# Expert weights loaded as paced halves, and shifted value tiles built without moving partitions

## The chip, the core and the metric

The kernel runs on one core of a Trainium2 chip. The metric is the device time of one execution in microseconds (us). Besides the DMA queues the core has five engines that the text names: PE (TensorE, the matrix multiplier; PEld is its weight load), DVE (VectorE), ACT (ScalarE), POOL (GpSimd) and SP (SyncE, which here only issues DMAs).

## What is computed

Three layers in float32, one after the other. Sizes: 4 batches, 8 heads, 512 local and 32 global tokens of 64 dimensions; 8 experts with 4 slots each; a last layer of width 2048.

```python
# 1. attention: a local token sees the 32 global tokens and the local ones within 32 positions
mask = np.abs(pos[:, None] - pos[None, :]) <= 32
s_ll = np.where(mask, scale * q_l @ k_l.T, -1e9)
a_l = softmax(concat([scale * q_l @ k_g.T, s_ll]))
out_l = a_l @ concat([v_g, v_l])          # global tokens see everything: out_g
# 2. soft mixture of experts on x (2176 tokens of 512)
logits = x @ phi
slot_input = softmax(logits, axis=0).T @ x
slot_out[e] = relu(slot_input[e] @ w1[e]) @ w2[e]
x = softmax(logits, axis=1) @ slot_out
# 3. last layer
out = relu(x @ w_in) ** 2 @ w_out
```

w_in and w_out are float64 in memory and are taken apart on the chip.

## The kernel before

**Stages.** The attention takes the first 166 us, the experts' matmuls follow up to about 202, and from there to the end (434 us) the last layer runs. The change touches the attention stage only, and the loading of expert weights that runs under it.

**Attention.** The 32 pairs of batch and head fall into 8 groups g of four heads (NG = 8), and the 512 query rows of a group into 4 units uu of 128 rows. That gives 32 steps n = 4g + uu. A unit has 16 / 4 = 4 blocks i of 32 queries; block i looks at a window of three key blocks x0, x0+1, x0+2 with x0 = first_block(i), and at the 32 global keys, 128 score columns in all. `emit_S` (L358) makes the scores on PE (32 matmuls of 32 x 128 a step), adds the mask on DVE (L376) and exponentiates on ACT (L380). `emit_T` transposes the result on PE (L388) and copies it on ACT. `emit_PV` multiplies by the values (L400) and divides on DVE (L407 to L409). `glob_S`, `glob_T` and `glob_PV` do the global queries (L423 to L471).

**Keys and values.** Keys lie in `kT` as six frames f of 128 columns: 32 global keys, then 96 local ones (three blocks). A window that starts inside a frame runs on into the next frame, whose global columns then stand in its middle: a contiguous run of 128 columns from 32 * (4f + (0, 2, 3)[x % 3]) holds the window, with its blocks rotated, and the mask is rotated likewise in `constants` (L293). Values lie in `v_e` the same way, by partitions: frame f has the global values on partitions 0 to 31 and three local blocks on 32 to 127. For a window with x % 3 == 0 the frame itself serves. For the others a shifted copy is made whose rows are in the order of the score columns: `prep_win` (x % 3 == 1, POOL, L343 and L344, two copies of 64 partitions) and `prep_win2` (x % 3 == 2, two windows at once, DVE, L350 and L352, four copies of 32 partitions x 520 numbers, each to another 32 partitions than it reads). `prep_win2` runs twice a group, so 16 times and 64 copies in all.

**Order of work.** Each piece is entered with a number (`at(when, ...)`), and the sorted list is the program order of PE, ACT, DVE, POOL and SP alike; nothing is reordered later. The unit of `when` is a step. In a group, counted from 4g, the loads of queries and keys for heads to come stand at 0.455 (first pair of heads, `load0`) and at 2.906 (second pair, right after `sort0`, the DVE copy L242 that reads the first pair at 2.901); the load of values stands at 3.675 (SP for the global part, POOL for the local one). A load that waits on SP holds up every load behind it.

**Expert weights.** 32 tiles of 1 MB, listed in `specs` in the order in which the experts use them. The first 13 go to slots of a ring that are free from the start (`more_weights`, L153), at the steps of the table WAT plus 0.9: 2.9, 3.9, 5.9, 7.9, 9.9, 10.9, 13.9, 14.9, 15.9 (twice), 18.9, 19.9 (twice). The next ones take slots that the attention gives back (`release`: three at 25.85, and so on).

Of the kernel before, what the change touches and what calls it, by code (L numbers as in the profile page):

```python
# [9 lines left out]
F32 = mybir.dt.float32  # L10
# [48 lines left out]
EX = 'act'  # L59
EE = 'act'  # L60
EW = 'act'
WAT = [2, 3, 5, 7, 9, 10, 13, 14, 15, 15, 18, 19, 19]
RECTS = 'A0-1 B0-2 C0-4 A2-6 B3-8 C5-10 A7-12 B9-15 A13-15 C11-15'
RING = 13
MORE = 5
# [8 lines left out]
def kernel(  # L74
# [7 lines left out]
    nc = tc.nc  # L82
    const = ctx.enter_context(tc.tile_pool(name="const", bufs=1))
    ring = ctx.enter_context(tc.tile_pool(name="ring", bufs=RING, side="right"))
# [19 lines left out]
    specs = []  # L104
    for kind, q in UNITS:
        es = slice(2 * q, 2 * q + 2)
        for m in range(4):
            src = (
                w1[es, m * 128:(m + 1) * 128, :].rearrange("e p f -> p e f") if kind == "w1" else
                w2[es, m * 256:(m + 1) * 256, :].rearrange("e (p t) d -> p e (t d)", t=2)  # L110
            )
# [4 lines left out]
    wt, raw = {}, {}  # L116
    w_in32, w_out32 = w_in.bitcast(I32), w_out.bitcast(I32)
    st = {"next": 0, "limit": RING}

    def slot(tag, shape, dt, nm):  # L120
        return ring.tile(shape, dt, tag=tag, name=nm, bufs={"w": RING, "k": MORE, "m": LAST}[tag])

    def load_raw(f, tag="k", halves=(0, 1)):
        if 0 in halves:
            raw[f] = slot(tag, [128, 2048], I32, "raw")
            nc.sync.dma_start(
                out=raw[f][:, 0:1024].rearrange("p (k w) -> p k w", k=4),
                in_=w_in32[:, 256 * f:256 * f + 256].rearrange("(k p) w -> p k w", p=128),
            )
        if 1 in halves:  # L130
            nc.sync.dma_start(out=raw[f][:, 1024:2048], in_=w_out32[128 * f:128 * f + 128, :])

    def more_weights(n=1):
        for _ in range(n):
            i = st["next"]
            if i >= len(specs) or i >= st["limit"]:
                return
            key, src = specs[i]
            if i == ALL:

                wt[key] = bp.tile([128, NT * 128], F32, tag="cT", name="extra")[:, 0:2048].rearrange(
                    "p (e f) -> p e f", e=2
                )
                nc.sync.dma_start(out=wt[key], in_=src)
                st["next"] += 1
                continue
            j = (i - (i > ALL)) % ALL
            if key[0] == "raw":
                load_raw(0, "w", [key[1]])
                st["next"] += 1  # L150
                continue
            t = slot("w" if j < RING else "k" if j < RING + MORE else "m", list(src.shape), F32, f"ring{i}")
            nc.sync.dma_start(out=t, in_=src)  # L153
            wt[key] = t
            st["next"] += 1

    def release(n):
        st["limit"] += n
        more_weights(n)
# [27 lines left out]
    kT, qT, v_e, kgT, qgT = [[], []], [[], []], [None] * 2, {}, {}  # L187
# [26 lines left out]
    pt_buf, win = [None] * 2, {}  # L214
# [4 lines left out]
    win = {x: w.rearrange("p (h d) -> p h d", d=65) for x, w in win.items()}  # L219
# [62 lines left out]
    def first_block(i):  # L282

        return min(max(i - 1, 0), 13)

    def constants(uu):

        for s in range(4):
            i = 4 * uu + s
            x0 = first_block(i)  # L290
            rows = slice(32 * s, 32 * s + 32)
            for x in range(x0, x0 + 3):
                c = (1 + x % 3 - (0, 2, 3)[x0 % 3]) % 4  # L293
                t = mask[rows, uu, 32 * c:32 * c + 32]
                if abs(x - i) > 1:
                    nc.gpsimd.memset(t, BIG)
                elif x != i:
                    nc.gpsimd.affine_select(
                        out=t, in_=t, pattern=[[i - x, 32]], compare_op=ALU.is_ge, fill=BIG, base=0,
                        channel_multiplier=x - i,  # L300
                    )
# [38 lines left out]
    def prep_win(g, x):  # L340

        ve, f = v_e[g % 2], x // 3
        nc.gpsimd.tensor_copy(win[x][0:64], ve[64:128, f])  # L343
        nc.gpsimd.tensor_copy(win[x][64:128], ve[0:64, f + 1])  # L344

    def prep_win2(g, k):
        ve, f = v_e[g % 2], 2 * k
        t = win2[1 if g == NG - 1 else k]
        win.update({3 * f + 2: t[:, 0], 3 * f + 5: t[:, 1]})
        nc.vector.tensor_copy(t[0:32], ve[96:128, f:f + 2])  # L350
        for c in range(3):
            nc.vector.tensor_copy(t[32 * c + 32:32 * c + 64], ve[32 * c:32 * c + 32, f + 1:f + 3])  # L352

    xb = {}
    P_t, PT_t = {}, {}

    def emit_S(g, uu):
        n = 4 * g + uu  # L358
        pt = p_buf[n % 2].rearrange("p (h x) -> p h x", h=4)
        nm = ap2.tile([128, 4], F32, tag="nm", name="nm", bufs=3)  # L360
        ps = [ps_s.tile([128, 2, 128], F32, tag="S", name="s") for _ in range(2)]
        for p in range(2):
            for hx in range(2):
                rows = slice(64 * hx, 64 * hx + 64)
                for s in range(4):
                    i = 4 * uu + s
                    x = first_block(i)
                    k0 = 32 * (4 * (x // 3) + (0, 2, 3)[x % 3])
                    nc.tensor.matmul(  # L369
                        ps[hx][32 * s:32 * s + 32, p, :],  # L370
                        qT[g % 2][p][rows, 32 * i:32 * i + 32], kT[g % 2][p][rows, k0:k0 + 128],
                        start=True, stop=True,
                    )
        for h in range(4):
            dst = pt[:, h, :]
            nc.vector.tensor_tensor_reduce(  # L376
                out=dst, in0=ps[h % 2][:, h // 2, :], in1=mask[:, uu, :], scale=1.0, scalar=FAR,
                op0=ALU.add, op1=ALU.min, accum_out=nm[:, h:h + 1],
            )
            nc.scalar.activation(out=dst, in_=dst, func=AF.Exp, bias=nm[:, h:h + 1], scale=-1.0)  # L380
        P_t[n] = pt
# [258 lines left out]
    load_global(k_g, "kg_sb")  # L640
    nc.gpsimd.memset(mask, 0.0)
    constants(0)
    ones()
    for uu in range(1, 4):
        constants(uu)
# [32 lines left out]
    def at(when, fn, *args):  # L678
        order.append((when, len(order), fn, args))

    steps = 4 * NG
    for n in range(steps):
        g, uu = n // 4, n % 4
        at(n - 2 + 0.1, emit_S, g, uu)
        at(n - 1 + 0.2, emit_T, g, uu)
        at(n + 0.6, emit_PV, g, uu)
    for g in range(NG):
        b, gq = g // 2, g % 2
        a = lambda name: 4 * g + (LASTPOS.get((name, g)) or POS[name])
        for p in range(2):  # L690
            for i, name in enumerate("qk"):
                at(-3 + 0.2 * p + 0.1 * i if g == 0 else a(f"sort{p}"), sort_qk, g, p, i)
            if (g, p) == (0, 0):
                at(-2.5, prep_global, "kg_sb", kg2, 1.0)
            for i, fn in enumerate((prep_q, prep_k)):
                at(-3 + 0.2 * p + 0.1 * i + 0.05 if g == 0 else 4 * g - 4 + p + 0.3 + 0.1 * i, fn, g, p)
            if g:
                at(-2.75 if (g, p) == (1, 0) else a("load0") if p == 0 else a("sort0") + 0.005, load_qk, g, p)
        at(a("glob_S"), glob_S, g)
        at(a("glob_T"), glob_T, g)  # L700
        at(a("glob_PV"), glob_PV, g)
        if g + 2 < NG:
            at(a("glob_PV") + 0.02, load_v, g + 2)
        for x in (1, 4, 7, 10, 13):
            at(a(f"w{x}"), prep_win, g, x)
        for k in range(2):
            at(a(f"v{k}"), prep_win2, g, k)
        if gq == 0:
            continue
        for uu in range(4 if g < NG - 1 else 2):  # L710
            at(a(f"x{uu}"), lambda b=b, uu=uu: x_T(b, uu, xb[(b, uu)], uu in (0, 3)))
        if g < NG - 1:
            at(a("L"), logits, b, b == 0, [(lt_all[:, b, :], slice(0, 128))])
            at(a("E"), slot_E, b)
            at(a("sl"), lambda b=b: slots(b, [xb[(b, uu)] for uu in range(4)]))
# [5 lines left out]
    at(2.19, slot_sums)  # L721
    at(steps - 2 + 0.8, lambda: x_T(B - 1, "g", x_g))
    at(steps - 1 + 0.5, last_xT, B - 1)
    for when in WAT:
        at(when + 0.9, more_weights)
    for when, n in RELEASE:
        at(when, release, n)
    for when, n in BUSYS:
# [163 lines left out]
    t = slot("m", [128, 4, 512], I32, "sgvm")  # L892
# [127 lines left out]
    t = slot("m", [128, 4, 512], I32, "sgvm2")  # L1020
# [169 lines left out]
    for n in range(len(seq)):  # L1190
        credit = min(credit + RATE, 1.2)
        if pieces and n >= START and min(free) <= n:
            kind, f, a, fs = pieces[0]
            if n >= due[kind, f] or (credit >= 1 and not ntile[max(n - 1, -1)]):
                d = 2
# [4 lines left out]
                d = min(d, late)  # L1200
# [59 lines left out]
```

## Time and profile before

| | us |
|---|---|
| median of 3 runs | 432.5 (431.55 to 434.31) |
| the profiled execution, its own time | 436.24 |
| its span, first to last instruction | 434.3 |
| PE busy / DVE busy / ACT busy / POOL busy in the span | 397.0 / 306.9 / 291.7 / 69.2 |
| mean granted clock of PE | 0.981 |

Busy is time in which an engine works on something; a wait or an issue of a DMA is not counted. Matmuls are pipelined and their ends are modelled, so a busy PE need not be at its peak. [...] In the views a row names the line, the engine, the operation, and the tile that is written and those that are read (out<-in).

### The profile page before, as it was taken

To read this page: it belongs to the slowest core of one execution; us is meant where nothing else is said; L and a number is where in the kernel's file an instruction comes from. 1 tells how busy PE (TensorE), PEld (TensorE's weight loads), DVE (VectorE), ACT (ScalarE), POOL (GpSimd) and SP (SyncE) were. 2 spreads that over 40 slices of the span, in tenths; PEclk is the share of its full clock that TensorE was granted. 3 is DMA by queue.
4 is the path that set the end of the run, shared out by engine and by line. 5 is a ranking of instruction groups with operands and counts; after the bars stand their busy time and mean duration, and the time that the engine had idled before them with its cause. 6 is when DMAs were issued, how large, how long until landed. Compare 5 with 4: busy or idle time off the path is not lost.

```text
span 434.3 us, 11765 instructions
## 1 busy us (share of the span) xinstructions
PE 397.0 (91%) x4530; PEld 289.9 (67%) x4530; DVE 306.9 (71%) x928; ACT 291.7 (67%) x692; POOL 69.2 (16%) x169
## 2 busy tenths in 40 slices
PE   6968888887889889999889999999999999999995
PEld 5747565564566654335667777878788787888883
DVE  2878779775987852436989996897788686735523
ACT  3556777693778761114888898878689786866670
POOL 7326346261743201000000000000000000000000
PEclk9988999996999999999999999999999999999998
DMA  7667696786878698999622232314020000003303
GB/s 184 148 197 208 213 296 204 261 223 236 200 225 258 217 361 339 394 407 375 230 98 97 78 117 54 140 26 169 0 97 2 0 1 2 0 2 145 138 9 121
DMA packets 46247, 70.29 MB, mean 162 GB/s; under 512 B 16336, under 2 KB 32720, under 8 KB 46192
## 3 DMA queue, kind: packets, MB, share of 16 engines
q1 hardware_dynamic: 44560, 66.40, 45.2%
q0 software_dynamic: 1632, 3.15, 3.1%
q8 instruction: 36, 0.59, 0.5%
q14 instruction: 19, 0.16, 0.1%
HBM read 65.08 MB, written 4.46 MB: 160 GB/s over the span
## 4 chain that ended last, share of the span: by engine, by line
PE 69%; DVE 11%; ACT 8%; DMA 5%; issue 4%; SPq 1%; POOL 0%; DVEq 0%; ACTq 0%; POOLq 0%
PE ops L1063 14%; PE ops L1064 14%; PE ops L1065 14%; PE hps L1028 4%; DMA qk<-in_k_l_dram 4%; PE hp L841 3%; PE so L869 3%; PE X L400 2%; PE s L369 2%; DVE tbuf L352 2%; ACT pbuf L380 2%; PE pT L388 2%; DVE pbuf L376 2%; DVE qk L242 1%; DMA v<-in_v_g_dram 1%
## 5 line engine op out<-in xcount | busy, mean ns | idle before, releaser
L1063 PE MATMUL ops<-hl,gh 128*128 128x512 f32 x266 | 105.8, 398 | 0.1
L1064 PE MATMUL ops<-hl,gh 128*128 128x512 f32 x266 | 105.5, 397 | 0.0
L1065 PE MATMUL ops<-hl,gl 128*128 128x512 f32 x266 | 105.0, 395 | 0.4 <-DVE gl L1052 0.4
L1052 DVE TENSOR_TENSOR gl<-r,gh 128x384 fp32r<-128x384 f32 x96 | 50.0, 531 | 28.1 <-ACT r L1047 27.9
L380 ACT ACTIVATE pbuf<-pbuf,nm 128x128 f32<-128x128 f32 x128 | 40.9, 390 | 34.1 <-DVE nm L376 33.7
L1035 ACT ACTIVATE r<-hps 128x384 f32<-128x384 f32 x96 | 45.1, 470 | 24.6 <-PE hps L1028 23.2
L1065 PEld LDWEIGHTS ops<-hl,gl 128*128 128x128 f32 x266 | 50.1, 188 | 13.2 <-DVE gl L1052 0.9
L1063 PEld LDWEIGHTS ops<-hl,gh 128*128 128x128 f32 x266 | 49.9, 188 | 12.1 <-ACT oacc L1075 0.7
L1064 PEld LDWEIGHTS ops<-hl,gh 128*128 128x128 f32 x266 | 50.0, 188 | 8.0
L1047 ACT ACTIVATE r<-r 128x384 f32<-128x384 f32 x96 | 48.7, 507 | 3.0
L1043 ACT ACTIVATE gh<-r 128x384 fp32r<-128x384 f32 x96 | 48.6, 506 | 2.6
L1028 PE MATMUL hps<-cT,wst 128*128 128x384 f32 x96 | 33.6, 353 | 2.1 <-ACT r L1035 2.0
L376 DVE CUSTOM_DVE_ANT_0 pbuf<-s,tbuf 128x128 f32<-128x128 f32 x128 | 29.4, 286 | 8.3 <-PE s L369 7.1
L1079 DVE SCALAR_TENSOR_TENSOR oacc<-ops,oacc 128x512 f32<-128x512 f32 x38 | 24.7, 686 | 4.1 <-PE ops L1065 4.0
L921 DVE SCALAR_TENSOR_TENSOR sgvm<-raw,sgvm 128x512 int32<-128x512 int32 x32 | 22.0, 686 | 5.3 <-ACT sgvm L915 5.3
L388 PE MATMUL pT<-ident,pbuf 128*128 128x128 f32 x128 | 22.1, 298 | 2.9 <-ACT tbuf L163 2.9
L1028 PEld LDWEIGHTS hps<-cT,wst 128*128 128x128 f32 x96 | 17.9, 188 | 9.5 <-ACT r L1035 2.7
L257 POOL DMA_DIRECT2D v<-in_v_l_dram x36 | 23.7, 665 | 0.0
L915 ACT ACTIVATE sgvm<-sgvm,ebias 128x512 int32<-128x512 int32 x32 | 22.8, 712 | 0.5 <-DVE sgvm L909 0.3
L918 DVE SCALAR_TENSOR_TENSOR sgvm<-raw,sgvm 128x512 f32<-128x512 uint32 x32 | 22.0, 686 | 0.1
L388 PEld LDWEIGHTS pT<-ident,pbuf 128*128 128x128 f32 x128 | 14.5, 147 | 9.1 <-ACT tbuf L163 3.9
L976 DVE TENSOR_TENSOR wst<-wpr,misc 128x256 fp32r<-128x256 f32 (+1 forms) x10 | 3.7, 372 | 18.3 <-ACT misc L971 18.3
(201 smaller groups left out, 710.2 us busy)
## 6 DMA issues: line engine op xcount, KB each, us to landing
ring<-in_moe_w_dram SPq DMA_DIRECT2D x31, 1024.0 KB, 8.6
raw<-in_moe_w_in_dram SPq DMA_DIRECT2D x16, 512.0 KB, 4.2
raw<-in_moe_w_out_dram SPq DMA_DIRECT2D x16, 512.0 KB, 5.0
out_dram<-oacc SPq DMA_DIRECT2D x16, 256.0 KB, 2.1
qk<-in_q_l_dram SPq DMA_DIRECT2D x15, 256.0 KB, 3.5
qk<-in_k_l_dram SPq DMA_DIRECT2D x15, 256.0 KB, 4.4
v<-in_v_l_dram POOLq DMA_DIRECT2D x30, 96.0 KB, 4.7
v<-in_v_g_dram SPq DMA_DIRECT2D x48, 32.0 KB, 3.9
```

Of the source, the lines that this page charges most:

```text
L376: nc.vector.tensor_tensor_reduce(out=dst, in0=ps[h % 2][:, h // 2, :], in1=mask[:, uu, :], scale=1.0, scalar=FAR, op0=ALU.add, op1=ALU.min ...
L380: nc.scalar.activation(out=dst, in_=dst, func=AF.Exp, bias=nm[:, h:h + 1], scale=-1.0)
L388: nc.tensor.transpose(ps[:, 128 * h:128 * h + 128], pt[:, h, :], ident)
L1028: nc.tensor.matmul(ps, wst[:, f, :], cT[:, t0:t0 + n], start=True, stop=True)
L1035: nc.scalar.activation(out=r, in_=ps, func=AF.Relu)
L1043: nc.scalar.activation(out=gh, in_=r, func=AF.Square)
L1047: nc.scalar.activation(out=r, in_=r, func=AF.Square)
L1052: eng.tensor_tensor(out=gL, in0=sq, in1=gh.bitcast(F32), op=ALU.subtract)
L1063: nc.tensor.matmul(ob[tt], gh[:, s], hi, start=first, stop=False)
L1064: nc.tensor.matmul(ob[tt], gh[:, s], lo, start=False, stop=False)
L1065: nc.tensor.matmul(ob[tt], gL[:, s], hi, start=False, stop=last)
L1079: nc.vector.scalar_tensor_tensor(out=t, in0=ps, scalar=WS, in1=t, op0=ALU.mult, op1=ALU.add)
```

## The change

Four edits that hang together.

1. **Value tiles.** In `prep_win` and `prep_win2` a row of values stays on its partitions: the blocks that lie in the next frame are copied from there, the others from this frame. `prep_win2` needs two copies (96 and 32 partitions) in place of four, 32 in all in place of 64; `prep_win` still takes two.
2. **Score columns.** The rows of the value tiles now stand in the order global, block 0, 1, 2 of a frame, so the score columns must too. `window_keys` reads the keys for a window with x % 3 == 1 as two runs of 64 columns and for x % 3 == 2 as four runs of 32, the later address first (steps of -64 and -96). Of the 16 blocks of a group 6 have x % 3 == 0 and stay one run, 6 have two runs and 4 have four. The mask goes to the same columns in `constants`.
3. **Expert loads.** The 13 loads of the ring become 26 loads of half a tile (0.5 MB; `ring_halves`). The table PACE puts them later: from step 4.9 to 25.71 where WAT had 2.9 to 19.9. In each group k = 1 to 5 one half stands at 4k + 0.9, two at 4k + 1.71, and two (k = 1, 2) or one (k = 3 to 5) at 4k + 2.76; four more halves follow at 24.9 and 25.71.
4. **Pacing.** The halves at .71 and .76 wait for POOL: a memset of one number in the slot stands ahead of each in POOL's order, and SP's load waits for it.

```diff
--- before.py
+++ after.py
@@ -59,7 +59,8 @@
 EX = 'act'
 EE = 'act'
 EW = 'act'
-WAT = [2, 3, 5, 7, 9, 10, 13, 14, 15, 15, 18, 19, 19]
+PACE = [(4 * k + d, n, w) for k in range(1, 6) for d, n, w in ((0.9, 1, False), (1.71, 2, True), (2.76, 2 if k < 3 else 1, True))]
+PACE += [(24.9, 2, False), (25.71, 2, True)]
 RECTS = 'A0-1 B0-2 C0-4 A2-6 B3-8 C5-10 A7-12 B9-15 A13-15 C11-15'
 RING = 13
 MORE = 5
@@ -154,6 +155,24 @@
             wt[key] = t
             st["next"] += 1
 
+    part = {}
+
+    def ring_halves(n, paced):
+
+        for _ in range(n):
+            key, src = specs[st["next"]]
+            c = part.get("c", 0)
+            if c == 0:
+                part["t"] = slot("w", list(src.shape), F32, f"ring{st['next']}")
+            t = part["t"]
+            if paced:
+                nc.gpsimd.memset(t[0:1, c, 0:1], 0.0)
+            nc.sync.dma_start(out=t[:, c:c + 1], in_=src[:, c:c + 1])
+            part["c"] = 1 - c
+            if c:
+                wt[key] = t
+                st["next"] += 1
+
     def release(n):
         st["limit"] += n
         more_weights(n)
@@ -290,7 +309,7 @@
             x0 = first_block(i)
             rows = slice(32 * s, 32 * s + 32)
             for x in range(x0, x0 + 3):
-                c = (1 + x % 3 - (0, 2, 3)[x0 % 3]) % 4
+                c = 1 + x % 3
                 t = mask[rows, uu, 32 * c:32 * c + 32]
                 if abs(x - i) > 1:
                     nc.gpsimd.memset(t, BIG)
@@ -340,19 +359,26 @@
     def prep_win(g, x):
 
         ve, f = v_e[g % 2], x // 3
-        nc.gpsimd.tensor_copy(win[x][0:64], ve[64:128, f])
-        nc.gpsimd.tensor_copy(win[x][64:128], ve[0:64, f + 1])
+        nc.gpsimd.tensor_copy(win[x][0:64], ve[0:64, f + 1])
+        nc.gpsimd.tensor_copy(win[x][64:128], ve[64:128, f])
 
     def prep_win2(g, k):
         ve, f = v_e[g % 2], 2 * k
         t = win2[1 if g == NG - 1 else k]
         win.update({3 * f + 2: t[:, 0], 3 * f + 5: t[:, 1]})
-        nc.vector.tensor_copy(t[0:32], ve[96:128, f:f + 2])
-        for c in range(3):
-            nc.vector.tensor_copy(t[32 * c + 32:32 * c + 64], ve[32 * c:32 * c + 32, f + 1:f + 3])
+        nc.vector.tensor_copy(t[0:96], ve[0:96, f + 1:f + 3])
+        nc.vector.tensor_copy(t[96:128], ve[96:128, f:f + 2])
 
     xb = {}
     P_t, PT_t = {}, {}
+
+    def window_keys(kt, x):
+
+        f, r = x // 3, x % 3
+        if not r:
+            return kt[:, 128 * f:128 * f + 128]
+        dims = [[-64, 2], [1, 64]] if r == 1 else [[-64, 2], [-96, 2], [1, 32]]
+        return bass.AP(kt.tensor, kt.offset + 128 * (f + r), [list(kt.ap[0])] + dims)
 
     def emit_S(g, uu):
         n = 4 * g + uu
@@ -364,11 +390,9 @@
                 rows = slice(64 * hx, 64 * hx + 64)
                 for s in range(4):
                     i = 4 * uu + s
-                    x = first_block(i)
-                    k0 = 32 * (4 * (x // 3) + (0, 2, 3)[x % 3])
                     nc.tensor.matmul(
                         ps[hx][32 * s:32 * s + 32, p, :],
-                        qT[g % 2][p][rows, 32 * i:32 * i + 32], kT[g % 2][p][rows, k0:k0 + 128],
+                        qT[g % 2][p][rows, 32 * i:32 * i + 32], window_keys(kT[g % 2][p][rows], first_block(i)),
                         start=True, stop=True,
                     )
         for h in range(4):
@@ -721,8 +745,8 @@
     at(2.19, slot_sums)
     at(steps - 2 + 0.8, lambda: x_T(B - 1, "g", x_g))
     at(steps - 1 + 0.5, last_xT, B - 1)
-    for when in WAT:
-        at(when + 0.9, more_weights)
+    for when, n, paced in PACE:
+        at(when, ring_halves, n, paced)
     for when, n in RELEASE:
         at(when, release, n)
     for when, n in BUSYS:
```

Three places show how the instructions move.

DVE, in the steps of group 5 (heads 4 to 7 of batch 2). The line numbers of the changed file are 19 to 24 higher; q_99 is a slot that holds a shifted value tile (win2), v_104 a frame tile of values. Before:

```order
L376 ISA nm 128x1
L350 COPY q_99<-v_104 32x520
L352 COPY q_99<-v_104 32x520 x3
L407 TENSOR_SCALAR rc<-X 128x4
L408 RECIPROCAL rc<-rc 128x4
```

and after the change:

```order
L400 ISA nm 128x1
L369 COPY q_99<-v_104 96x520
L370 COPY q_99<-v_104 32x520
L431 TENSOR_SCALAR rc<-X 128x4
L432 RECIPROCAL rc<-rc 128x4
```

Four copies are two, one of them three times as tall; what stands ahead and behind is the same.

SP, from the load of global values for group 6 to the next load of values. qk is the one buffer for queries and keys as loaded, ring_N is a weight slot. Before:

```order
L254 DMA v_100<-in_v_g_dram 32x4x64 x6
L153 DMA ring_2271<-in_moe_w_dram 128x2x1024
L153 DMA ring_2273<-in_moe_w_dram 128x2x1024
L235 DMA qk<-in_q_l_dram 128x2x256
L235 DMA qk<-in_k_l_dram 128x2x256
```

(then the same two qk loads for the second pair of heads, and L254 again). After:

```order
L273 DMA v_100<-in_v_g_dram 32x4x64 x6
L254 DMA qk<-in_q_l_dram 128x2x256
L254 DMA qk<-in_k_l_dram 128x2x256
L170 DMA ring_2342<-in_moe_w_dram 128x1024 x2
L170 DMA ring_2418<-in_moe_w_dram 128x1024 x2
```

(then the second pair's qk loads and L273). Two weight tiles that stood ahead of the first pair's load now stand behind it, and ahead of the second pair's.

POOL, in the same group. The tiles named gbuf, tbuf and v_104 hold value windows made by prep_win. Before:

```order
L343 COPY v_104<-v_104 64x260
L344 COPY v_104<-v_104 64x260
L431 MEMSET gbuf 128x5x32
L343 COPY gbuf<-v_100 64x260
L344 COPY gbuf<-v_100 64x260
```

and after:

```order
L362 COPY v_104<-v_104 64x260
L363 COPY v_104<-v_104 64x260
L169 MEMSET ring_2342 1x1
L169 MEMSET ring_2418 1x1
L455 MEMSET gbuf 128x5x32
L362 COPY gbuf<-v_100 64x260
L363 COPY gbuf<-v_100 64x260
L169 MEMSET ring_2418 1x1
```

The three memsets are what three of the four halves of that group wait for, so these halves leave SP when POOL has come that far.

## Rows read from the trace of the kernel before

**Rows 1.** The page: the profiled span.

```profile
span 434.3 us, 11765 instructions
```

**Rows 2.** Busy time in three stretches; the last columns are clock, DMA share, GB/s.

```profile
10.00:165.90 155.90, 130.67 (x3146) 93.97 (x3145) 121.62 (x543) 105.27 (x313) 60.04 (x126) 0.96 0.74 235
165.90:202.00 36.10, 35.88 (x297) 12.41 (x297) 14.33 (x59) 7.30 (x12) 1.52 (x2) 1.00 0.98 376
210.00:434.30 224.30, 216.18 (x994) 171.04 (x986) 163.07 (x313) 170.48 (x352) 0.00 (x0) 0.99 0.20 68
```

**Rows 3.** Waits of PE from 10 to 166: us in total, times, longest.

```profile
PE X L400 <- DVE xb L409: 2.6, 3, 1.5
...
PE s L369 <- issue: 2.2, 1, 2.2
...
PE X L400 <- issue: 1.6, 2, 0.9
...
PE Xg L459 <- issue: 1.4, 1, 1.4
```

**Rows 4.** DVE's copies by form, 10 to 166: count | busy us, mean ns | idle before.

```profile
L352 DVE COPY tbuf<-v 32x520 f32<-32x520 f32 x27 | 14.6, 540 | 0.5
...
L242 DVE COPY qk<-qk 128x512 f32<-128x512 f32 x28 | 11.6, 453 | 0.3 <-DMA qk<-in_k_l_dram 0.3
...
L352 DVE COPY q<-v 32x520 f32<-32x520 f32 x21 | 10.4, 496 | 0.3
...
L350 DVE COPY tbuf<-v 32x520 f32<-32x520 f32 x9 | 4.6, 511 | 0.3
...
L350 DVE COPY q<-v 32x520 f32<-32x520 f32 x7 | 3.1, 444 | 0.2
```

**Rows 5.** Timeline of DVE, one call of prep_win2: start us, us.

```profile
29.24 0.57 DVE L350 COPY q<-v 32x520 f32<-32x520 f32 x1
29.82 1.63 DVE L352 COPY q<-v 32x520 f32<-32x520 f32 x3
```

**Rows 6.** Chain that ended last, 10 to 166, share of it by line.

```profile
by line: issue 10.5%; DMA qk<-in_k_l_dram 10.0%; PE X L400 6.4%; PE s L369 6.1%; DVE tbuf L352 5.8%; ACT pbuf L380 4.5%; PE pT L388 4.5%; DVE pbuf L376 4.5%; DVE qk L242 3.0%; DMA v<-in_v_g_dram 3.0%; PE sl L548 3.0%; PE sg L423 2.5%; PE Xg
```

**Rows 7.** SP's timeline, the chain and DVE's timeline around one load of keys.

```profile
113.50 1.12 SPq L153 DMA_DIRECT2D ring<-in_moe_w_dram  x2
...
116.23 9.91 DMA qk<-in_k_l_dram
...
126.17 0.59 DVE L242 COPY qk<-qk 128x512 f32<-128x512 f32 x1 [0.26 <-DMA qk<-in_k_l_dram]
```

**Rows 8.** A stop of PE: its timeline, busy time after it, DMA queues 96 to 101.

```profile
100.69 1.11 PE L369 MATMUL s<-keys,pbuf 64*32 64x128 f32 x32 [2.19 <-issue]
...
102.00:104.00 2.00, 2.00 (x37) 1.49 (x37) 1.94 (x11) 1.76 (x5) 0.03 (x1) 0.50 0.98 381
...
q8 instruction: 1, 0.02, 1.4%
```

**Rows 9.** Matmuls by form, 43.6 to 145.7, and 166 to 202 (L869).

```profile
L369 PE MATMUL s<-keys,q 64*32 64x128 f32 x384 | 9.7, 276 | 2.6 <-ACT xT L163 2.6
...
L423 PE MATMUL sg<-keys 64*32 64x480 f32 x56 | 7.1, 575 | 0.0
...
L869 PE MATMUL so<-ring,hTz 128*32 128x512 f32 x128 | 15.7, 598 | 0.0
```

**Rows 10.** Timelines of POOL, SP and DVE around one second-pair load.

```profile
49.36 0.40 POOL L344 COPY gbuf<-v 64x260 f32<-64x260 f32 x1
...
50.66 0.37 SPq L235 DMA_DIRECT2D qk<-in_q_l_dram  x1
...
57.69 0.96 DVE L242 COPY qk<-qk 128x512 f32<-128x512 f32 x2
```

**Rows 11.** The page: loads to landing; busy time 140 to 150.

```profile
qk<-in_k_l_dram SPq DMA_DIRECT2D x15, 256.0 KB, 4.4
...
140.00:150.00 10.00, 8.92 (x261) 5.49 (x250) 8.44 (x42) 7.19 (x21) 2.65 (x7) 1.00 0.66 254
```

## The prediction, made before the changed kernel was timed

> **What bounds the kernel now.** I read the span first [rows 1], then the busy time by stage [rows 2]. The reader is to see three stages with different limits. From 210 to the end PE is busy 216.2 of 224.3 us, with the DMA at 0.20: the last layer is PE's, and no instruction of it changes. From 166 to 202 PE is busy 35.9 of 36.1 us while the DMA works at 0.98: PE is fed just fast enough. So only the attention can give something: 155.9 us in which PE is busy 130.7 and DVE 121.6. Neither is full; they take turns being late, since every step passes from PE to DVE to ACT and back to PE. PE's idle time there is 155.9 - 130.7 = 25.2 us, and that is the most that the change can give as long as PE's own work stays as it is.
>
> PE's waits divide this [rows 3]. Three rows, 2.2 + 1.6 + 1.4 = 5.2 us, end in "issue": PE stood still though no semaphore held it. The other 20.0 us are mostly waits for DVE and ACT, such as 2.6 us for the division on DVE (L409). DVE's value copies stand ahead of it. They are 64 copies, 14.6 + 10.4 + 4.6 + 3.1 = 32.7 us, 0.51 us each [rows 4], and they come as a block of four, 29.24 to 31.45, in front of the division [rows 5]. The chain of work that ended last passes through the copies of one line into one tile for 5.8% of 156 us, 9.0 us of the 14.6 us that these copies are busy [rows 4, 6].
>
> **The change part by part.**
>
> Value copies. 32 copies go, 32 stay. The trace has no copy of 96 partitions; bounds for it are the shortest mean of the 32-partition copies, 0.444 us, and the longest, 0.540; a copy of 128 partitions x 512 numbers takes 0.453 us, so height costs nothing here [rows 4]. With 0.51 as before DVE loses 32 x 0.51 = 16.4 us of work; with the bounds 32.7 - 32 x 0.540 = 15.4 to 32.7 - 32 x 0.444 = 18.5. How much of that reaches the end: nothing, if PE and ACT fill the gap with their own lateness, and all of it at most (it is below the 20.0 us of waits). The chain holds 9.0 us of the one row; half of it goes, 4.5 us. For the other 18.1 us of copies I assume half that share of the chain, 31%, so 5.6 us, of which half goes, 2.8. That makes 7.3; some of it will be lost to another engine that is late next (ACT, busy 105 us, or PE itself), and I take 6.0 us.
>
> Expert loads, the collisions. The chain shows a load of keys of 9.91 us from 116.23, behind two 1 MB loads that were issued at 113.50 [rows 7]; the median load of keys lands after 4.4 us [rows 11]. It looks like a gain of 5 us, but it is none: DVE, which reads the keys, was idle for 0.26 us only when they landed [rows 7]. In the new order no half stands ahead of the first pair's load, so this load lands sooner and a faster DVE does not run into it. I count 0.
>
> Expert loads, the stops of PE. From 98.5 to 100.69 PE stood for 2.19 us ahead of score matmuls that nothing held; between 96 and 101 one packet of the instruction queue q8 was moved, and from 102 to 104 the DMA still worked at 0.98 [rows 8]. [...] My reading is that a full DMA delays PE's instructions, and that halves with pauses between them leave gaps. [...] I take 2.0 of the stops and 1.0 of the clock, the part of one stop.
>
> Score columns in pieces. The 32 score matmuls of a step stay, at 0.276 us each with several under way at once; 10 of 16 blocks now read 2 or 4 runs. The trace has such a read: the global scores (L423) take 480 columns as five runs of 96, in 0.575 us, 1.20 ns a column, and the experts' matmul (L869) takes 512 columns in one run in 0.598 us, 1.17 ns a column [rows 9]. Runs cost 0.03 ns a column, or nothing. I take 0; the other bound is in the rivals.
>
> Pacing. 19 memsets of one number join POOL, which is busy 60 of 156 us [rows 2]: hidden. SP issues 26 loads in place of 13, and waits in order. Behind the half at 4k + 2.76 stands the second pair's load. At the place of k = 1 POOL ends the copies that would stand ahead of that memset at 49.76, and SP issued the load at 50.66; DVE reads it at 57.69, 7 us later [rows 10], against 4.4 us for a landing [rows 11]. Two halves ahead, 1 MB at the 376 GB/s of [rows 2], are 2.8 us, so the spare 2.6 us are just used up, and less so with one half (k = 3 to 5). Bounds 0 and about 1 us for each of five groups; I take 0, since the halves leave before SP may issue the load.
>
> Later loads. Two tiles more are loaded after step 24.9. They stand ahead of three tiles for the slots given back at 25.85. The DMA is at 0.66 from 140 to 150 [rows 11], 3.4 us idle, enough for 1.3 MB, and the tiles that come later are used later; the first 13 are all in before the experts start. If that cover were gone, 0.7 MB would be late by 2 us. I take 0.
>
> **Sum.** 6.0 + 2.0 + 1.0 = 9.0 us less. The profiled execution took 436.24 us, 1.9 around its span of 434.3: its span would be 425.3 and its time 427.2. It lies 3.7 us above the median of 432.5, perhaps by just such a stop, which the median run may not have; against the median 9.0 less is 423.5. I put 424.
>
> **Rivals.**
>
> PE takes over. The step is also bound by PE's 130.7 us and by the hand-over between engines, so that a shorter DVE block only lets DVE wait longer. For it: PE is the busier of the two [rows 2]. Against it: PE's idle time is mostly for DVE and ACT. Then a third of the copies' 6.0 us stays, and 0.5 for the stops: 2.5 less, 430.
>
> All of it counts. The 16.4 us come through nearly whole, or 11 of them with the stops and the low clock gone (11 + 5 = 16): 416.5. For it: DVE's blocks of copies are followed by PE's waits; against: the chain holds little more than half of them.
>
> Slower: runs cost on PE. If a read of several runs is slow in a 128-column matmul, with runs of 32 and backward steps that the five runs of 96 do not have, the 32 score matmuls of a step get longer in 10 of 16 blocks. 384 of them keep PE busy for 9.7 us [rows 9], since they overlap, so all 1024 for 26 us, and the 10 in 16 for 16 us. At twice the time that is 16 us more on PE, which would then be the bound: 432.5 - 9 + 16 = 439.5. It decides from a factor of 1.6 on (9 / 16), and makes the kernel over 1% slower from 1.8 on. [...] The row of L423 against L869 shows no such cost for runs of 96; no row here has runs of 32.
>
> Not as meant. The halves do nothing for PE's stops, because these have another cause or because SP, held until POOL comes by, then issues several halves in a row. Only the copies count: 6.0 less, 426.5. For it: no row joins the packet of q8 with the stop [rows 8]. Against it: two of the three stops are short, and the longest lies in a full DMA. [...]
>
> **How the numbers follow.** The forecast, 419 to 426: 0.37. Not as meant, around 426.5: 0.18. PE takes over, 428 to 432: 0.24. All of it counts, below 419: 0.13. Runs cost on PE, or the second pair's loads come late, over 432: 0.08. The range of 8 in 10 leaves out the lower half of the fourth and most of the last: 416 to 432. 1% is 4.3 us, about what a measurement of this kernel can tell from no change. Faster, below 428.2: 0.37 + 0.13, most of the second (0.15) and a little of the third, 0.67. Within 1%, up to 436.8: the rest of these two and a little of the last, 0.27. Slower: 0.06.
>
> **What would show it.** In the changed profile: 32 copies at 0.45 to 0.54 us, the 96-partition ones no longer than the others; DVE's busy time in the attention near 105 us; score matmuls at 0.276 us as before (at 0.35 and more the runs cost); no stop of PE over 2 us that ends in "issue", and fewer windows at a clock of 0.50; the experts' first matmul near 157 in place of 166, with nothing changed in the 268 us behind it. I would be wrong if PE's busy time in the attention grew, if DVE waited for keys (L242 on the second pair), or if PE waited for a weight tile in the experts' stage.

## The result, and the profile after

The changed kernel takes 430.4 us (median of 20 runs), the kernel before beside it 433.6 us (20 runs). The ratio is 0.991, with a 95% interval of 0.989 to 0.994: 3.8 us faster, where 9 were forecast. (Ratios leave out a kernel's runs that lie over 1.5% above its fastest, medians hold all runs; by the medians the gain here is 3.1 us.) A repeat gave 0.990 (0.987 to 0.994). The forecast of 424.0 was wrong in size; its range, 416 to 432, holds the time.

The profiled execution of the changed kernel, first from its page (busy time and share of each engine, number of instructions), then by stage:

```profile
span 428.4 us, 11784 instructions
PE 391.8 (91%) x4530; PEld 286.9 (67%) x4530; DVE 290.7 (68%) x896; ACT 291.5 (68%) x692; POOL 68.8 (16%) x188
```

```profile
core 0: us, PE busy (x) PEld busy (x) DVE busy (x) ACT busy (x) POOL busy (x), PEclk, DMA share, GB/s
10.00:159.60 149.60, 125.03 (x3145) 91.10 (x3144) 105.89 (x511) 104.72 (x311) 59.62 (x145) 0.98 0.80 243
159.60:195.70 36.10, 35.84 (x297) 12.36 (x297) 14.00 (x59) 7.29 (x12) 1.52 (x2) 1.00 1.00 383
203.70:428.40 224.70, 216.29 (x994) 171.10 (x987) 163.01 (x313) 170.49 (x352) 0.00 (x0) 1.00 0.20 68
```

Against [rows 2] the attention is 149.6 us long and not 155.9, with DVE 15.7 us less busy; the two other stages are what they were. These two executions lie 5.9 us apart in span [rows 1], more than the medians: the time of a kernel spreads over some 8 to 10 us from run to run (425.8 to 436.0 here), and a single trace is one draw from that.

The new copies and the score matmuls, by form (count | busy us, mean ns | idle before):

```profile
L370 DVE COPY tbuf<-v 32x520 f32<-32x520 f32 x9 | 4.8, 536 | 0.1
L369 DVE COPY tbuf<-v 96x520 f32<-96x520 f32 x9 | 4.0, 448 | 0.0
L370 DVE COPY q<-v 32x520 f32<-32x520 f32 x7 | 3.3, 466 | 0.2
L369 DVE COPY q<-v 96x520 f32<-96x520 f32 x7 | 3.2, 450 | 0.3 <-issue 0.3
L393 PE MATMUL s<-keys,pbuf 64*32 64x128 f32 x512 | 12.2, 275 | 2.6 <-issue 2.5
```

The 32 copies take 15.3 us where 64 took 32.7 [rows 4]. Three quarters of the partitions took no longer here (0.448 and 0.450 us) than one quarter (0.536 and 0.466). Score matmuls take 0.275 us where the keys are one run or two and 0.276 us where they are four (384, 384 and 256 records in this trace), as with one run before [rows 9]. (A float32 matmul has two records in a trace, 1024 for the 512 score matmuls of the program: the 32 score matmuls of a step, in the text above, are the records of 16.)

What did not come as forecast stands in the waits of the attention, PE's and then DVE's (us in total, times, longest):

```profile
PE X L424 <- issue: 4.8, 5, 2.3
PE s L393 <- issue: 4.6, 4, 1.5
PE Xg L483 <- issue: 2.0, 1, 2.0
```

```profile
DVE rc L431 <- PE X L424: 10.8, 9, 2.7
DVE qk L261 <- DMA qk<-in_k_l_dram: 3.2, 5, 1.0
```

PE's stops that no semaphore explains are 4.8 + 4.6 + 2.0 = 11.4 us and not 5.2 [rows 3]. DVE now waits for keys, 3.7 us with the queries' 0.5 (0.3 before). And DVE's freed time shows as waiting for PE's value matmuls, 10.8 us (3.9 before).

### The profile page after: what moved, and what is told of

Same layout as the page of the kernel before. It is cut to its first block, busy times and chain, and to the rows that moved or that the text cites. A ratio compares the mean times of both kernels' runs of the same rounds, so it can differ in the third digit from the quotient of the medians.

```text
span 428.4 us, 11784 instructions
## 1 busy us (share of the span) xinstructions
PE 391.8 (91%) x4530; PEld 286.9 (67%) x4530; DVE 290.7 (68%) x896; ACT 291.5 (68%) x692; POOL 68.8 (16%) x188
## 4 chain that ended last, share of the span: by engine, by line
PE 74%; ACT 7%; DVE 7%; DMA 7%; issue 5%; SPq 0%; DVEq 0%; ACTq 0%
PE ops L1087 14%; PE ops L1088 14%; PE ops L1089 14%; PE hps L1052 4%; PE hp L865 4%; DMA qk<-in_k_l_dram 3%; PE so L893 3%; PE s L393 3%; PE X L424 3%; PE pT L412 2%; ACT pbuf L404 1%; DMA v<-in_v_g_dram 1%; PE sg L447 1%; DMA keys<-in_q_l_dram 1%; PE wpp L988 1%
## 5 line engine op out<-in xcount | busy, mean ns | idle before, releaser
L412 PE MATMUL pT<-ident,pbuf 128*128 128x128 f32 x128 | 21.2, 289 | 2.3 <-ACT tbuf L182 2.3
L412 PEld LDWEIGHTS pT<-ident,pbuf 128*128 128x128 f32 x128 | 14.1, 143 | 7.9 <-ACT tbuf L182 3.1
L261 DVE COPY qk<-qk 128x512 f32<-128x512 f32 x30 | 12.7, 446 | 7.6 <-DMA qk<-in_q_l_dram 4.1
```

The lines of the kernel that those rows point to most:

```text
L412: nc.tensor.transpose(ps[:, 128 * h:128 * h + 128], pt[:, h, :], ident)
```

## The experiments

Three theories were put against each other. F, later P: the copies are worth what was forecast or more, but PE's stops grow and take it back. K: the keys behind the halves take it back. C: the copies are simply worth less, since the next engine is as late. The edits are cut to the lines that matter.

**One half of the change at a time.** copies_only has the new copies and score columns with the 13 whole tiles of before; halves_only has the old copies with the halves.

```
copies_only:  - for when, n, paced in PACE: at(when, ring_halves, n, paced)
              + for when in WAT: at(when + 0.9, more_weights)
halves_only:  before.py, with PACE and ring_halves in place of WAT
```

> The changed copies and score columns with the old loads (13 whole tiles at the old steps). Three theories of why the change gave 3.8 us and not 9. Theory F (full queue): the halves did not end PE's unexplained stops but spread them (5.2 us of stops of 0.7 us and more before, 11 us after), so the copies alone should give the 6 us that I had counted, 427 to 428 against 433.5, with PE stops of about 5 us as before. Theory K (keys late): the halves that go out ahead of the second pair's keys make DVE wait (3.7 us in the changed kernel, 0.3 before), so again the copies alone give about 6 us, and DVE's waits for keys fall under 1 us. Theory C (copies worth less): DVE's saved time is taken up by the next engine, the halves change nothing, and the copies alone give the same as the whole change, 429 to 430.

> The old value copies and score columns with the new loads (26 paced halves). Theory F: slower than before by 2 to 3 us, with more PE stops than before, 10 us in sum. Theory K: slower by about 2 us, with DVE waiting 3 us for the second pair's keys. Theory C: no change, within 1 us of before.

copies_only: 431.2 us, ratio 0.994 (0.991 to 0.998), 2.5 us faster. halves_only: 436.7 us, ratio 1.000 (0.996 to 1.005). So the halves give nothing by themselves. By the ratio they cost nothing either, but the median of all twelve runs is 3.2 us above before's, as F expected, so that stays open. DVE did not wait for keys in halves_only, against K, and PE's stops were 7.8 us:

```profile
PE X L419 <- issue: 6.6, 5, 2.3
PE s L388 <- issue: 0.6, 1, 0.6
PE Xg L478 <- issue: 0.6, 1, 0.6
```

The copies alone give 2.5 us, nearest to C. But the trace of copies_only is not what C would have. PE's waits there:

```profile
PE X L405 <- issue: 6.4, 5, 2.9
PE s L374 <- issue: 6.1, 5, 3.1
PE Xg L464 <- issue: 1.3, 1, 1.3
```

13.8 us of stops under the old loads, against 5.2 with the old copies under the same loads [rows 3].

**The keys ahead of the halves.**

```
keys_first:  - (2.76, 2 if k < 3 else 1, True)
             + (2.92, 2 if k < 3 else 1, True)
```

> The changed kernel with the last one or two halves of each group behind the load of the second pair's keys and not ahead of it. Theory K: 2 to 3 us faster than the changed kernel, 427 to 428.5, DVE's waits for the second pair's keys under 1 us. Theories F and C: as the changed kernel, 430 to 431, the stops of PE still near 11 us.

431.6 us, ratio 0.992 (0.989 to 0.996): as the changed kernel. DVE's waits for keys fell from 3.7 to 0.4 us, and PE's stops were 13.2 us. K falls: that wait was real, but taking it away is worth nothing as long as PE stops.

**No expert loads in the attention, first try.** All tiles are asked for behind the attention's last loads.

```
quiet:  - st = {"next": 0, "limit": RING}
        + st = {"next": 0, "limit": RING + 7}
        - RELEASE = ((25.85, 3), (27.75, 1), (29.15, 1), (30.85, 2))
        + RELEASE = ()
        - for when, n, paced in PACE: at(when, ring_halves, n, paced)
        + at(31.2, more_weights, 20)
```

> The changed kernel with all loads of expert tiles put behind the attention's last steps, so that the queues hold only the attention's own loads while it runs. The experts then wait for their tiles, so that only the attention is read here: its last instruction of the sums on DVE, which fell at about 159 us in the changed kernel. Theory F: PE's stops that end in issue fall from 11 us to under 2 us and the attention ends 8 to 10 us earlier. Theory K: the stops stay, DVE's waits for keys vanish, and the attention ends 3 to 4 us earlier. Theory C: the attention ends where it did, within 2 us.

In the one run (439.8 us) the attention ended at 155.6 us (the experts' first matmul; 159.6 in the changed kernel), 4 us earlier and not 8 to 10. The cause is that nothing held SP back, and the tiles came from about 110 us on. That makes one execution with two parts, by busy time and DMA share:

```profile
core 0: us, PE busy (x) PEld busy (x) DVE busy (x) ACT busy (x) POOL busy (x), PEclk, DMA share, GB/s
20.00:110.00 90.00, 79.85 (x2166) 57.68 (x2166) 73.58 (x358) 70.02 (x210) 45.55 (x96) 1.00 0.47 117
110.00:150.00 40.00, 30.71 (x746) 21.66 (x745) 23.15 (x109) 25.48 (x76) 10.25 (x23) 0.96 0.99 362
```

With the DMA at 0.47 there is no stop of PE over 0.6 us in 90 us. With the DMA at 0.99 there are four in 26 us: 2.22 us at 121.33, 1.13 us at 146.54, and these two from PE's timeline (start, us, instruction, count, [idle before]):

```profile
127.76 0.44 PE L393 MATMUL s<-keys,pbuf 64*32 64x128 f32 x12 [1.77 <-issue]
133.74 1.01 PE L393 MATMUL s<-keys,pbuf 64*32 64x128 f32 x18 [1.59 <-issue]
```

**No expert loads in the attention, held.** Now a memset on DVE behind the attention's last sum stands ahead of the first tile, and SP waits for it. The experts then wait for tiles, so the times are far above the others and only the pair is read.

```
held_new, held_old:  as quiet, but with limit RING + 9, more_weights(ALL) behind
                     last_sums() in place of the at(31.2, ...), no release(2), and
+            if i == 0:
+                nc.vector.memset(t[0:1, 0, 0:1], 0.0)
             nc.sync.dma_start(out=t, in_=src)
```

> The changed kernel with every load of an expert tile held back until the attention's last sum on DVE, so that the queues are nearly free while the attention runs; the experts then wait for their tiles, and the time is the attention plus a constant. It is read against held_old alone. Theory P: DVE's 16 us are worth in the attention what I had counted, but with the queues full PE stands still at its instruction supply just when DVE no longer keeps it waiting. Then with free queues the stops are under 2 us, the attention ends near 150, and held_new is 6 to 8 us below held_old. Theory C: the saved copies lie beside the next engine's work, with or without loads: held_new is 2.5 to 4 us below held_old, as copies_only was below before.

> The kernel before with the same hold on the experts' loads. It is the other half of the pair: theory P has the attention end near 157, 6 to 8 us later than in held_new, with PE waiting for DVE and not at issue; theory C has it 2.5 to 4 us later.

held_new 470.2 us (469.6 to 472.1), held_old 480.6 us (478.9 to 482.0): 10.4 us for the same edit that was worth 2.5 with the tiles in the queue. The two attentions by busy time, new and old, and the last matmuls of each:

```profile
10.00:148.00 138.00, 123.36 (x3151) 90.06 (x3150) 105.11 (x512) 103.89 (x313) 59.13 (x126) 0.99 0.42 105
...
147.71 0.38 PE L646 MATMUL pz<-zsum,rsum 128*128 128x1 f32 x2 [0.83 <-DVE zsum L644]
153.84 1.93 PE L865 MATMUL hp<-ring,siT 128*32 128x512 f32 x8 [5.74 <-DMA ring<-in_moe_w_dram]
```

```profile
10.00:160.00 150.00, 124.26 (x3144) 90.91 (x3142) 122.33 (x544) 104.76 (x311) 60.45 (x126) 0.99 0.38 96
...
160.04 0.38 PE L641 MATMUL pz<-zsum,rsum 128*128 128x1 f32 x2 [0.83 <-DVE zsum L639]
166.20 1.93 PE L860 MATMUL hp<-ring,siT 128*32 128x512 f32 x8 [5.77 <-DMA ring<-in_moe_w_dram]
```

The new attention ends at 148, the old one at 160. Of PE's waits for issue one is left in held_new, and none in held_old:

```profile
PE s L395 <- issue: 0.2, 1, 0.2
```

C falls: the copies lie on the path. That was more than the 6 to 8 us expected. The five runs of each also lie within 2.5 and 3.1 us, where the kernels with whole tiles or halves in the attention spread over 6.0 to 10.7 us (in 4 to 29 runs).

**Still fewer copies.** 24 of the 32 copies are left out (the six middle groups keep the first group's shifted tiles).

```
few_copies, in prep_win2:  +        if 0 < g < NG - 1:
                           +            return
```

> The changed kernel, its loads as they are, with the value copies of the six middle groups left out (24 of the 32 copies, 11.5 us of DVE; the shifted tiles keep the first group's values, so the output is not the reference's). Theory P: with the queues full it gains little more, 1 to 2 us below the changed kernel, while PE's stops that end in issue stay at 10 us and more. Theory C with a third of DVE's time on the path: 4 us below it, 426 to 427. If DVE still were the bound: 9 to 11 us below it.

430.9 us, ratio 0.994 (0.990 to 0.998): 11.5 us less on DVE, and nothing gained, less even than the 1 to 2 us of P. PE's stops were 8.5 us, and DVE, now ahead, ran into the loads of keys, which was not expected:

```profile
DVE rc L433 <- PE X L426: 15.3, 12, 2.7
DVE qk L261 <- DMA qk<-in_q_l_dram: 9.2, 4, 3.0
DVE qk L261 <- DMA qk<-in_k_l_dram: 2.3, 4, 1.1
```

**All halves earlier.**

```
early_all:  - 2 if k < 3 else 1          + 2
            - (24.9, 2, False), (25.71, 2, True)   + (24.9, 1, False)
```

> The changed kernel with two halves in every group's last place, so that 25 of 26 halves are sent by the sixth group and one is left for step 24.9, in place of four. In the changed kernel the queues were full from 132 to 146 and PE stopped for 2.3 us at 145.26. Theory P: less is waiting then, the stop near 145 shrinks under 1 us, and the time is 1 to 2 us below the changed kernel, 428.5 to 429.5. Theory C: as the changed kernel, 430.4, within 1 us.

Four runs, one of 424.6 us and three of 434.0 to 435.3: unclear, and none of them where it was expected. In the longest of the four, which was the profiled one, the stop near the end shrank to 0.67 us as expected, but others grew (3.24 us at 56.54), 10.1 us in all. Nothing on the time follows from it.

**What the stops are.** Their places in PE's program can be counted. In the trace a float32 matmul has two records and a transpose one (1024 of L393 for 512 matmuls, 128 of L412 for 128 transposes); counted so, the stops of 0.7 us and more of the changed kernel come after 719, 844, 969, 1219, 1345, 1469, 2845 and 2970 records. That is 94 + 125 x k (719, 844, 969, 1219, 1344, 1469, 2844, 2969) within 1. Those of before come after 469, 719, 1219 and 1844, on the same grid. All 82 stops over 0.55 us in the 14 traces with stops lie within 2 of the grid; places without a rule would lie within 2 one time in 25 (5 of 125). The profile's page has 4530 matmul records and as many weight loads on PE, and this row of it counts the packets of the queue q8:

```profile
q8 instruction: 36, 0.59, 0.6%
```

4530 / 36 = 126 matmul records for each packet of 16 KB, and 0.59 MB / 9060 = 65 bytes for each instruction: q8 brings PE's instructions, and PE stops where the block of one packet ends.

The times of q8's packets, which the traces record too, show what ends a stop. Each of the 82 stops ends 1.24 to 1.66 us after a packet has landed, while a new packet comes only every 5 to 6 us on average: PE stands until the next block is there. Moving the packet itself takes 1.1 to 1.2 us on average in every trace. What differs is when it lands, counted from PE's start on the block before, and how soon PE is through with that block (means over 21 blocks between records 469 and 3094, one trace each; the stops are not counted in the block):

| | PE is through after | the next packet lands after | spare, with 1.4 us from landing to start |
|---|---|---|---|
| before (whole tiles) | 5.62 us | 3.85 us | 0.4 us |
| copies_only (whole tiles) | 5.01 us | 3.79 us | -0.2 us |
| held_old (no tiles) | 5.53 us | 2.33 us | 1.8 us |
| held_new (no tiles) | 5.03 us | 2.15 us | 1.5 us |

The loads make the packet land 1.5 to 1.6 us later, with either copies. The new copies bring PE to the block's end 0.5 to 0.6 us sooner, and that uses up the spare time.

To test whether the grid is counted from the program's start or belongs to the work, 34 matmuls (68 records) were put at PE's start, where it waits for the first loads anyway. (The expectation counts matmuls of the program, one each; in records its places are the grid above.)

```
shift:  - BUSY0 = 6
        + BUSY0 = 40
```

> The changed kernel with 34 matmuls more on the identity at PE's start, where PE waits for the first loads. PE's stops that end in issue stood, in six kernels with the loads in the attention, at matmuls 410, 477, 546, 615, 688, 758, 826, ... and 1664 of PE's program, 65 to 73 apart. Theory P (the stops are PE's own supply of instructions, which comes in blocks of fixed length): the grid stays at the same numbers counted from the program's start, so that the stops fall 34 matmuls earlier in the work, at 376, 512, 654, 1630 by the old count. If a stop belonged to the work itself (a tile, a load that has just been issued), it would stay at 410, 546, 688 and 1664 by the old count, ahead of the same instruction as before. The time is no part of it: 430 to 433.

The stops stayed on the grid as counted from the start, at 1846, 2096, 2721 and 2846, within 2 of it, where a stop that belonged to the work would have moved by 68. The one at 2845 stood in the score matmuls in the changed kernel and in eight others (first row); now it stands ahead of them, inside the global value matmuls (second fence), with the instruction that used to be hit running freely. Only these four stops of over 0.5 us were in this one execution (434.0 us), so those at 1630 and 512 of the expectation could not be seen.

```profile
138.70 0.59 PE L393 MATMUL s<-keys,pbuf 64*32 64x128 f32 x18 [1.00 <-issue]
```

```profile
132.90 1.00 PE L483 MATMUL Xg<-v,gbuf 128*32 128x65 f32 x43
136.31 0.31 PE L483 MATMUL Xg<-v,gbuf 64*32 64x65 f32 x5 [2.41 <-issue]
```

**Loads in smaller pieces.** Halves one at a time, then quarters, evenly spaced and each behind a one-number memset on DVE.

```
even:            + PACE = [(4.5 + 0.8 * j, 1, True) for j in range(26)]
even_quarters:   + PACE = [(4.5 + 0.4 * j, 1, True) for j in range(52)]
                 + e, h = c // 2, slice(512 * (c % 2), 512 * (c % 2) + 512)
                 + nc.sync.dma_start(out=t[:, e:e + 1, h], in_=src[:, e:e + 1, h])
```

> [...] No two halves stand in the queue together, and none of them is sent in the last seven steps. Theory P: the queue is full for shorter stretches, the stops of PE fall from 11 us to about 6, and the time falls by 2 to 5 us against the changed kernel, 425 to 428. If the stops depend on the amount that is moved and not on how it is bunched: as the changed kernel, 430 to 431.

> As the kernel with evenly sent halves, but 52 quarters of 256 KB, one every 0.4 steps. Theory P: as that one or 1 to 2 us faster, since what can stand ahead of PE's instructions is half as long. If the amount counts and not the bunching: 430 to 431, or 1 to 2 us slower for rows of 2 KB in place of 4 KB and 26 more memsets on DVE.

even: 430.9 us, ratio 0.992 (0.987 to 0.996). The time did not fall as expected. The stops were 5.3 us in the profiled execution, but that was the fastest of the ten (426.4 us), so they need not be those of the others; DVE's waits for keys were 5.7 us there. even_quarters: 426.6 us in four runs, ratio 0.984 (0.977 to 0.991; the interval overlaps that of even), with these stops:

```profile
PE s L393 <- issue: 3.6, 3, 1.3
PE Xg L483 <- issue: 0.3, 1, 0.3
PE X L424 <- issue: 0.2, 1, 0.2
```

Then the quarters with the old copies, and the two kernels again beside them.

```
quarters_old:  before.py, with the loads of even_quarters
```

> The old value copies and score columns with the 52 evenly sent quarters. Theory P (the copies' gain is eaten by PE's stops under a full queue, and 10.4 us of it are there when there are none): with fewer stops more of it is seen, so that this kernel is 6 to 8 us slower than the one with the new copies and the same quarters, about 433 against 426.5; the quarters alone then give nothing against before. If the quarters and the copies are worth their own amounts each, 2.5 to 4 us for the copies as in copies_only and the rest for the quarters: 429.5 to 430.5.

> The kernel with evenly sent quarters once more, to settle its size: 426 to 428, if the first four runs (423.7 to 428.5) hold.

> The changed kernel beside these two on the same chip: 430 to 431, a ratio of 0.99 to before; the quarters are 3 to 4 us faster than it.

quarters_old 432.7 us, ratio 0.997 (0.993 to 1.001). even_quarters again 427.0 us, 0.986 (0.982 to 0.990). The changed kernel again 430.1 us, 0.990 (0.987 to 0.994). So the quarters are 2 to 3 us faster than the changed kernel, a little less than expected and with intervals that overlap, and about 6.2 us faster than before: the fastest version here. With quarters the copies are worth 0.986 / 0.997, 4.9 us (5.7 by the medians), between the two answers that had been expected.

## Why the prediction was wrong

All loads together, with the worth of the copies from ratios (by the medians of all runs in brackets; the held pair by medians alone), and PE's stops and DVE's waits for keys between 10 and 160 us in one profiled execution each. A single trace is one draw: those of before and of halves_only come from executions 3 and 1 us longer than their medians.

| expert loads in the attention | copies worth | stops, old copies | stops, new copies | waits for keys, old, new |
|---|---|---|---|---|
| 13 whole tiles | 2.5 us (2.4) | 5.2 | 13.8 | 0.3, 4.5 |
| 26 halves | 4.0 us (6.3) | 7.8 | 11.4, 9.8 | 0, 3.7, 3.7 |
| 52 quarters | 4.9 us (5.7) | 2.6 | 4.1, 6.4 | 0.2, 2.2, 5.3 |
| none | 10.4 us | 0 | 0.2 | 0, 0.6 |

**The step that failed is "I take 2.0 of the stops": its sign, and that it was added to the copies' 6.0 as a term of its own.** Taken one at a time, the copies gave 2.5 us in place of 6.0, and the halves 0 (by the ratio) in place of 2.0 and 1.0. The stops were taken as something that the loads alone make, so that smoother loads shorten them. They are not independent of the copies: PE stops when it is through with one block of instructions and the next is still missing, and with faster copies it is through sooner (after 5.0 us and not 5.5 to 5.6). The stops grew by 6.2 us instead of falling by 2.0. Under the same whole tiles they went from 5.2 to 13.8 when only the copies changed (to 7.8 when only the loads changed), and with the queues free the copies gave 10.4. That 10.4 - 6.2 = 4.2 comes near the 3.8 measured is partly luck. Row by row, the growth of the stops covers what the copies lose against 10.4 with whole tiles (8.6 of 7.9 us), but only a part of it with halves (2.0 to 3.6 of 6.4) and quarters (1.5 to 3.8 of 5.5); DVE's waits for keys grew by 2 to 5 us in all three rows.

**Copies, 6.0.** The work that goes was right: 17.4 us, within the bounds of 15.4 to 18.5. Its worth on the path was put too low: half of what was on the chain, where 10.4 of 17.4 us come through when PE's instructions arrive. It was too high for the kernel as it is (2.5 us with whole tiles), since PE's supply takes most of it.

**The rival "PE takes over" gave the time, 430, but not for its reason.** It put the limit in PE's 130.7 us of work and in the hand-over. held_new does the same work in 138 us, of which PE is busy 123. What stands in the way with the loads present is PE's instructions, and behind them the keys. That the time fell into the range, through this rival, is luck.

**"All of it counts"** has its 11 us for the copies (10.4) only without tiles in the queues. **"Not as meant"** was right that the halves do not end the stops (7.8 us in halves_only), but wrong in doubting the cause: the forecast's own reading, that a full DMA delays PE's instructions, holds (landings after 3.8 us and not 2.2 to 2.3), and only its second half, that paced halves leave gaps, does not. The trace of before could already have been counted: 36 packets of q8 for 9060 instructions, and its four stops on the grid.

**"Runs cost on PE"** fell: 0.275 us with two runs and 0.276 with four, backward steps included, against 0.275 with one.

**The clock, 1.0.** No run shows this term, since none isolates the clock. What the traces of before and of the changed kernel show is a granted clock of 1.00 or 0.50 of full speed (0.50 from 102 to 104 us in before [rows 8], from 22 to 28 in the changed kernel), and 32 records of score matmuls that took 1.11 us at 0.50 [rows 8] and 0.67 us at 1.00 (from 107.10 in before). The mean granted clock of the attention was 0.98 against 0.96 [rows 2]; with these two levels that is 0.02 x 149.6 x 2 = 6.0 us at the lower one in place of 0.04 x 155.9 x 2 = 12.5. If half of it is lost, an estimate from these numbers and the most, this pair gives back up to 3.2 us, more than the term. Between 10 and 160 us the granted clock was 0.95 in before and also, with the new copies, in early_all, and 0.97 to 1.00 in the other fourteen traces, so nothing shows that the gain belongs to the change.

**Terms taken at 0.** Pacing: DVE did wait for the second pair's keys, which the prediction named as a sign against itself, but by keys_first that wait was worth nothing that its runs could tell. Later loads: the queues were full from 132 to 146 (1403 packets at 99.9%), where a stop of 2.34 us ends at 145.26, and early_all did not settle its price. The experts' stage ran as before, without a wait for a tile.

**The signs.** Right: copies of 0.448 to 0.536 us, DVE busy 105.9 us, score matmuls, 268.8 us behind the attention as before (268.4). Wrong: two stops over 2 us, and the experts' first matmul at 159.6 and not 157.

**What stays open.** That a faster DVE makes the stops longer rests on single traces, though the packets' times agree with the copies' worth. The sum of the stops is not the loss in time: keys_first has 13.2 us and the changed kernel 11.4 in nearly the same time. That few_copies adds no gain, with stops of 8.5 us, says that other supply, the keys, stands right behind. How the two share the loss was not separated. Even spacing alone gave nothing (even against the changed kernel), so what the quarters gave goes with their size; this rests on two ratios whose intervals overlap.

## What to carry to other kernels

Before a gain on one engine is added to a gain on another, see whether the second engine's lateness was hidden behind the first: here 17 us less of DVE uncovered PE's own supply of instructions, and of the 10.4 us that this is worth with free queues 2.5 were left. Where PE stands still for "issue", count its matmuls at each stop; if they lie on a grid as long as the instruction queue's packets, look at the DMA queues: here the stops ended with no tiles in them (0 and 0.2 us in all), and were shorter with smaller, spread loads (4.1 and 6.4 us with quarters, 11.4 in the changed kernel). To know what an edit is worth by itself, time it once with the background loads held back.

## What the runs showed of the hardware

The page lists PE's instructions among the DMA queues: 36 packets of q8 of 16 KB, one for 126 matmul records and their weight loads. With the expert loads in the queues the packet landed 3.3 to 4.1 us after PE had begun the block before, and in the held pair, with the DMA at 0.38 and 0.42 of its time, after 2.2 to 2.3 us. A crossing then stopped PE for up to 3.2 us; in the held pair none of some 24 crossings did for more than 0.2 us. The spread of run times was smaller without tiles in the attention, 2.5 and 3.1 us in 5 runs each, against 2.7 to 6.7 with quarters (4 to 12 runs) and 6.0 to 10.7 with halves or whole tiles (4 to 29 runs); more runs widen a spread, so this is a hint. A copy of 96 partitions took no longer than one of 32 (0.448 to 0.450 us and 0.466 to 0.536 us).
